# Output-bank copies, weight conversions and token sums emitted at other places in a fused attention and two-layer kernel

## The chip, the cores and the metric

One core of a Trainium2 chip runs the whole program. The metric is the device time of one execution in microseconds (us). The engines are TensorE (PE), VectorE (DVE), ScalarE (ACT), GpSimd (POOL) and SyncE (SP, which issues every DMA here). Each runs its own instructions in the order in which the program emitted them, and waits for semaphores of the others.

## The reference

A linear attention over 4 x 576 tokens (8 heads of 64), then a gated layer, then a softplus layer. All is float32 on the chip.

```python
q_s = softmax over d of q;  k_s = softmax over tokens of k
kv = einsum('bhsd,bhse->bhde', k_s, v);  x = einsum('bhsd,bhde->bhse', q_s, kv)   # 2304 x 512
xn = x / rms(x) * rms_g
x = (silu(xn @ w_gate) * (xn @ w_val)) @ w_out          # 512 -> 1536 -> 512
h = x @ w_in                                            # 512 -> 2048
out = softplus(h) @ w_out2                              # 2048 -> 512
```

## The kernel before

**Arithmetic.** A float32 factor is split in two parts, high and low, and a product is three matmuls (L728 to L730). So every weight and every activation has to be cast (high) and subtracted (low) before PE can use it. Weights arrive as 64-bit floats: a load into one of two `raw` buffers (`fetch`, L211), then a chain of steps on ACT and DVE (`stages`, L340): `convert_a` (absolute value, L246 or L250), `clamp` (L255, L261), `words` (L265, L269; it ends with `fetch(n + RAW)`, the load of the weight two places on), the cast `make_h` (L310 on ACT, L308 on POOL in the softplus layer), the subtraction `make_l` (L316). Weights that come in pairs pass through four sums (L330 to L333).

**Tiles and stages.** Tokens come in six blocks of 384. The first four feature blocks of the gated layer run as plain products in a hand-written list that also does the attention, and, for the last two token blocks, in a loop of eight steps (24 positions, below). The other eight feature blocks run in pairs, on pairs of token blocks, as seven products in place of eight, in 12 *units* (`u`, 0 to 11): each of the seven products is 6 matmuls for the gate and 6 for the value, and its factors are weight sums and *quads*, which are blocks or sums of blocks of the tokens (11, 21, t2, t1, t3, 22, t4). The softplus layer has 24 such units (`u`, 0 to 23), with one product of 6 matmuls each, and output products of 512 columns.

**Quads.** A *run* is a stretch of units on one pair of token blocks; run 0 is unit 0, run 1 is unit 1, run 2 is units 2 and 3. `quad_todo` lists what a run needs in the order of `MAKE`: a `sum` is one DVE subtraction (L986), usually in place over one of its blocks, a `split` is an ACT cast (L1003, L1006) and, at the next position, a low half (`quad_low`, L1016 for a whole place, L1019 twice for a place in two banks), on POOL for runs 1 and 2, else on DVE. A split needs a free place; the head of the list blocks what follows.

**Order of the work.** The emission order is a small planner's. After each half product comes `background(rate)`: one *position*. It adds `rate` to a credit of at most 1.0, emits at most one entry of `quad_todo`, and lets `convert_some` take one step of each conversion in progress (three at most) while the credit isn't negative; steps and sums take credit. `need` forces conversions whose weights are due. A unit of the gated layer has 14 positions, one of the softplus layer 26.

**Output products.** The output products of unit u (8 `parts` of 6 matmuls) are emitted during unit u + 1, one after each product (`more(1)`), the rest at the unit's end. Each part needs one of four PSUM banks that ACT first fills with the residual (`prepare`, L1165), and ACT copies its result out (L1175). A part's emission is followed by the `prepare` of the part two places on. PSUM banks of the gate and value products are freed by ACT copies (L1252), by DVE additions (L1255, then L1259 and ACT's cast L1234 and POOL's low half L1235 for a hidden tile) or, at the seventh product, by the activation L1263. In the softplus layer the addition is L1364. The last plain output (`o_last`) is copied out by DVE (L775).

Of the kernel before, what the change touches and what calls it, by code (L numbers as in the profile page):

```python
# [79 lines left out]
def linear_attention_swiglu_softplus_kernel(  # L80
# [31 lines left out]
    NBITS = 3  # L112
    BW = P
# [80 lines left out]
    raws = {}  # L194
    bits = {}
# [12 lines left out]
    order += pair_a(3)[:4] + pair_b(2, Y0 + Y1) + pair_b(3, H2 + Y0 + Y1) + pair_a(3)[4:]  # L208
# [4 lines left out]
    def fetch(n):  # L213
# [17 lines left out]
        raws[n] = raw  # L231

# [168 lines left out]
    now = [0]  # L401
    credit = [0.0]

    def convert_some(force=False):
        stuck = False
        if not jobs or (len(jobs) < NBITS and jobs[-1][3] > 0):
            n = next_job[0]
            if n < len(order) and n - NBITS not in bits:
                jobs.append([n, list(stages(n)), now[0], 0])
                next_job[0] += 1  # L410
# [327 lines left out]
    with tc.manual_schedule():  # L738
# [197 lines left out]
        apart = {}  # L936
        outside = {}
# [40 lines left out]
        def quad_op(r, what, name):  # L978
            layer, jp = runs[r]
            if what == "sum":  # L980
# [3 lines left out]
                if r == 0 and name in ("t3", "t4"):  # L984
                    apart[r, name] = late[0].tile([P, 2, T], F32, tag="hb", name="t", bufs=NH)
                nc.vector.tensor_tensor(out=block(r, name), in0=x, in1=y, op=ALU.subtract)  # L986
                credit[0] -= 0.9
                return True
# [21 lines left out]
        def quad_low(r, name, src, w, q):  # L1010

            layer, jp = runs[r]
            credit[0] -= 0 if r in (1, 2) else 0.9
# [6 lines left out]
            if layer == "a":  # L1020
# [7 lines left out]
                if r == 0:  # L1028
                    last = {"t2": 1, "t1": 0}.get(name)
                else:  # L1030
                    last = {"t3": 1, "t4": 0}.get(name)
# [3 lines left out]
        quad_todo = []  # L1035
        for r, (layer, jp) in enumerate(runs):
            if layer == "b" or jp not in made_a:
                quad_todo += [(r, *x) for x in MAKE]
            else:
                quad_todo += [(r, "load", x) for x in USE]  # L1040
# [33 lines left out]
        def background(rate, quads=1):  # L1074
            now[0] += 1
            credit[0] = min(credit[0] + rate, 1.0)
# [4 lines left out]
        for i in range(LS, NA):  # L1081
# [10 lines left out]
            background(1.4)  # L1092
# [13 lines left out]
            background(1.4)  # L1106
# [8 lines left out]
            background(1.4)  # L1115
# [4 lines left out]
        def h_tile():  # L1120
            made[0] += 1
            if made[0] % (NH + 2) < NH:
                return late[0].tile([P, 2, T], F32R, tag="hb", name="hb", bufs=NH)
# [19 lines left out]
        def o_last():  # L1143
# [5 lines left out]
            def part(m):  # L1149
                c = slice(m * P, (m + 1) * P)  # L1150
                mm3(acc[m][:, :T], w[:, 0, c], w[:, 1, c], h[:, 0], h[:, 1], False, True)
                x2_out(i, m, "V")
# [70 lines left out]
        for u in range(len(ORDER_A)):  # L1223
# [16 lines left out]
            for k, (wn, off, xname, b, new) in enumerate(SEVEN):  # L1240
# [3 lines left out]
                for n in "gv":  # L1244
# [23 lines left out]
                    if n == "v":  # L1268
                        if ends_run:
                            release(r, xname)  # L1270
                        if u % 3 == 2:
                            done = {1: ("gx1", "vx1"), 4: ("gx3", "vx3"), 5: ("x4",), 6: ("gx2", "vx2")}.get(k, ())
                            for x in done:
                                ring_done((x, p))
                    background(1.1)
                if u % 3 == 1 and k == 0 and u < 3:
                    pass
                more(1)
            more(8)
            if u == 0:  # L1280
                add_ahead(outputs, 2)
# [67 lines left out]
        for u in range(NPB * len(ORDER_B)):  # L1349
# [4 lines left out]
            for k, (wn, off, xname, b, new) in enumerate(SEVEN):  # L1354
# [18 lines left out]
                background(0.45)  # L1373
                more(2 if u == 0 and k < 2 else 1)
                background(0.45, 0)
            for _ in range(12):
                more(1)
                background(0.45, 0)
# [38 lines left out]
```

## Time and profile before

| what | value |
|---|---|
| median of three runs | 969.01 us (965.15 to 969.09) |
| the profiled execution, its span | 969.88 us, 968.1 us |
| PE, DVE, ACT, POOL busy | 902.3, 597.7, 487.4, 239.2 us |
| DMA | 203.5 MB, 210 GB/s over the span |
| mean granted clock of TensorE | 0.978 |

Busy shares are means over stages with different limits. The stage rows below are read first; the waits of PE and the queues around them second. A granted clock of 1.00 is 2.4 GHz; the mean of a stretch lies below it where part of it ran at 1.2 GHz. The "idle before" in a row's brackets is the time in which its engine stood still, with what ended it.

### The profile page before, as it was taken

The numbers are of one execution on the slowest core, as the hardware profiler recorded it, in microseconds if no ns is written. First come the engines' busy times: TensorE is split into PE (matmuls) and PEld (weight loads), VectorE is DVE, ScalarE is ACT, GpSimd is POOL, SyncE is SP. The second block draws the span as 40 slices with busy tenths as digits, with TensorE's granted clock in tenths as the row PEclk, the third lists the DMA queues.
The fourth block names the chain that finished last, engine by engine and source line by source line (L and its number), as shares of the span: only waits on it lengthen the run. The fifth ranks groups of instructions, "written<-read, shape, count | busy, mean of one in ns | idle before, by whom it ended". The sixth has DMA issues, their size and how long they took to land.

```text
span 968.1 us, 13616 instructions
## 1 busy us (share of the span) xinstructions
PE 902.3 (93%) x4840; PEld 842.3 (87%) x4840; DVE 597.7 (62%) x1013; ACT 487.3 (50%) x994; POOL 239.2 (25%) x215
## 2 busy tenths in 40 slices
PE   7799999999677999999999987799999999999997
PEld 7689999999677999899999886689888989898996
DVE  7999987765754788788888877941442223322221
ACT  4585634344456677667777852233443334333332
POOL 4666404111454112121112155761000000000000
PEclk9999999999988999999999998899999999999999
DMA  9974444332557598687597639887539565286501
GB/s 253 252 188 119 122 124 120 120 109 100 221 222 279 189 359 295 219 316 291 178 383 289 226 150 339 300 311 291 174 111 340 163 204 164 101 328 206 167 22 65
DMA packets 111235, 203.53 MB, mean 210 GB/s; under 512 B 30272, under 2 KB 71232, under 8 KB 111168
## 3 DMA queue, kind: packets, MB, share of 16 engines
q1 hardware_dynamic: 111168, 202.67, 62.5%
q8 instruction: 38, 0.62, 0.3%
q14 instruction: 29, 0.24, 0.1%
HBM read 155.19 MB, written 47.45 MB: 209 GB/s over the span
## 4 chain that ended last, share of the span: by engine, by line
PE 67%; DVE 16%; DMA 6%; ACT 5%; issue 4%; POOL 2%; DVEq 0%; SPq 0%; ACTq 0%; POOLq 0%
PE yacc L729 6%; PE yacc L730 6%; PE yacc L728 6%; PE h L730 5%; PE h L729 5%; PE h L728 5%; PE acc L728 4%; PE acc L729 4%; PE acc L730 4%; PE g L728 3%; PE g L730 3%; PE g L729 3%; PE v L728 3%; PE v L729 3%; PE v L730 3%
## 5 line engine op out<-in xcount | busy, mean ns | idle before, releaser
L1364 DVE TENSOR_TENSOR p<-h,p 128x384 f32<-128x384 f32 x72 | 39.9, 555 | 160.6 <-PE h L730 159.0
L728 PE MATMUL h<-quad,wb 128*128 128x384 f32 x336 | 114.1, 339 | 16.8 <-DVE p L1364 15.3
L729 PE MATMUL h<-quad,wb 128*128 128x384 f32 x336 | 114.9, 342 | 0.0
L730 PE MATMUL h<-quad,wb 128*128 128x384 f32 x336 | 114.9, 342 | 0.0
L1298 ACT ACTIVATE p<-p 128x384 f32<-128x384 f32 x72 | 37.8, 526 | 131.9 <-DVE p L1364 131.9
L728 PEld LDWEIGHTS h<-quad,wb 128*128 128x128 f32 x336 | 63.9, 190 | 26.1 <-DVE p L1364 17.0
L1361 ACT COPY p<-h 128x384 f32<-128x384 f32 x72 | 34.6, 481 | 102.8 <-PE h L730 101.8
L728 PE MATMUL yacc<-wb,hb 128*128 128x512 f32 x210 | 82.2, 392 | 1.7 <-ACT y L1314 1.7
L729 PE MATMUL yacc<-wb,hb 128*128 128x512 f32 x210 | 83.0, 395 | 0.0
L730 PE MATMUL yacc<-wb,hb 128*128 128x512 f32 x210 | 83.0, 395 | 0.0
L729 PEld LDWEIGHTS h<-quad,wb 128*128 128x128 f32 x336 | 63.5, 189 | 7.2
L728 PE MATMUL g<-quad,w 128*128 128x384 f32 x168 | 58.1, 346 | 10.8 <-ACT s L1263 6.0
L1235 POOL TENSOR_TENSOR hb<-p,hb 128x384 fp32r<-128x384 f32 x26 | 27.0, 1037 | 154.5 <-ACT hb L1234 115.4
L730 PEld LDWEIGHTS h<-quad,wb 128*128 128x128 f32 x336 | 63.7, 190 | 0.0
L728 PE MATMUL acc<-hb,w 128*128 128x384 f32 x136 | 47.9, 352 | 15.8 <-ACT acc L1165 15.6
L728 PE MATMUL v<-quad,w 128*128 128x384 f32 x168 | 57.9, 345 | 0.5 <-DVE p L1255 0.5
L729 PE MATMUL g<-quad,w 128*128 128x384 f32 x168 | 58.0, 345 | 0.0
L730 PE MATMUL g<-quad,w 128*128 128x384 f32 x168 | 58.0, 345 | 0.0
L729 PE MATMUL v<-quad,w 128*128 128x384 f32 x168 | 57.2, 341 | 0.0
L730 PE MATMUL v<-quad,w 128*128 128x384 f32 x168 | 57.0, 339 | 0.0
L728 PE MATMUL acc<-h,w 128*128 128x384 f32 x152 | 51.2, 337 | 2.8 <-ACT acc L1165 2.8
L269 DVE SCALAR_TENSOR_TENSOR bits<-raw,bits 128x512 int32<-128x512 int32 x62 | 51.5, 833 | 1.6
(202 smaller groups left out, 2503.3 us busy)
## 6 DMA issues: line engine op xcount, KB each, us to landing
wb<-kept SPq DMA_DIRECT2D x120, 512.0 KB, 5.3
quad<-outside SPq DMA_DIRECT2D x31, 768.0 KB, 6.6
kept<-ws SPq DMA_DIRECT2D x40, 512.0 KB, 4.7
raw<-in_moe_w_out_dram SPq DMA_DIRECT2D x26, 512.0 KB, 3.8
outside<-quad SPq DMA_DIRECT2D x13, 768.0 KB, 3.8
quad<-outside SPq DMA_DIRECT2D x22, 384.0 KB, 5.4
raw<-in_moe_w_in_dram SPq DMA_DIRECT2D x16, 512.0 KB, 4.7
outside<-quad SPq DMA_DIRECT2D x16, 384.0 KB, 2.4
```

The source lines that it names most:

```text
L269: nc.vector.scalar_tensor_tensor(out=b, in0=words[:, :, 0], scalar=29, in1=b, op0=ALU.logical_shift_right, op1=ALU.bitwise_or)
L728: nc.tensor.matmul(out=ps, lhsT=wh, rhs=xh, start=first, stop=False, skip_group_check=more)
L729: nc.tensor.matmul(out=ps, lhsT=wh, rhs=xl, start=False, stop=False, skip_group_check=more)
L730: nc.tensor.matmul(out=ps, lhsT=wl, rhs=xh, start=False, stop=last, skip_group_check=more)
L1235: nc.gpsimd.tensor_tensor(out=h[:, 1], in0=a, in1=h[:, 0].bitcast(F32), op=ALU.subtract)
L1298: nc.scalar.activation(out=ln, in_=src, func=AF.Softplus)
L1361: nc.scalar.copy(out=t, in_=bk[b])
L1364: nc.vector.tensor_tensor(out=t, in0=bk[b], in1=t, op=ALU.add)
```

## The change

- `convert_some` starts a conversion only when a clock that `background` advances (2.08 at a plain position, 1.55 in the gated units, 0.6 in the softplus units) has passed its load's emission by `LANDING` = 7.5; a forced start (`need`) doesn't look at it.
- In a gated unit `more(1)` comes after the value's half product and ahead of that position's `background`, in place of after it; the first unit prepares three banks ahead, not two.
- Run 1's sums t1, t3 and t2 are emitted among run 0's entries, behind its first five (in the plain steps); t1 and t2 go to tiles of their own (`hb`) in place of overwriting their blocks. Run 1's splits have a new order, and the place of one token block is freed after the split of 22, not t3.
- A low half on POOL takes 0.6 credit in place of none. The last plain outputs are copied by ACT, not DVE. The weights `y` of the fourth pair come behind its `o` weights in the order.

```diff
@@ -110,6 +110,7 @@
     NS = 3
     NH = 5
     NBITS = 3
+    LANDING = 7.5
     BW = P
     RAW = 2
     EARLY = ["x20", "x21", "x22", "x23", "xy3", "xy2"]
@@ -192,6 +193,7 @@
         ring_free.add(ring_of.pop(key))
 
     raws = {}
+    fetched = {}
     bits = {}
     def pair_a(p):
         return [(n, GA[0] + 2 * p + i) for n in "gvo" for i in range(2)]
@@ -205,7 +207,7 @@
     order = [(n, f) for f in range(GA[0]) for n in "gvo"] + pair_a(0)
     order += pair_a(1) + pair_b(0, H2 + Y0 + Y1)
     order += pair_a(2)[:4] + pair_b(1, H2 + Y0 + Y1) + pair_b(2, H2) + pair_a(2)[4:]
-    order += pair_a(3)[:4] + pair_b(2, Y0 + Y1) + pair_b(3, H2 + Y0 + Y1) + pair_a(3)[4:]
+    order += pair_a(3)[:4] + pair_b(2, Y0 + Y1) + pair_b(3, H2) + pair_a(3)[4:] + pair_b(3, Y0 + Y1)
     for p in range(4, NPB):
         order += pair_b(p, H2 + Y0 + Y1)
     assert len(order) == len(set(order)) == 3 * FA + 2 * FB
@@ -229,6 +231,7 @@
             src = {"g": w_gate, "v": w_val, "h": w2_in}[name]
             nc.sync.dma_start(out=r64.rearrange("p (k c) -> p k c", c=P), in_=src[:, c].rearrange("(k p) c -> p k c", p=P))
         raws[n] = raw
+        fetched[n] = clock[0]
 
     softplus = []
 
@@ -399,13 +402,14 @@
     jobs = []
     next_job = [NL]
     now = [0]
+    clock = [0.0]
     credit = [0.0]
 
     def convert_some(force=False):
         stuck = False
         if not jobs or (len(jobs) < NBITS and jobs[-1][3] > 0):
             n = next_job[0]
-            if n < len(order) and n - NBITS not in bits:
+            if n < len(order) and n - NBITS not in bits and (force or clock[0] >= fetched.get(n, 0.0) + LANDING):
                 jobs.append([n, list(stages(n)), now[0], 0])
                 next_job[0] += 1
         for job in list(jobs):
@@ -934,6 +938,16 @@
         hl_out = [-1, -2, -3]
         hl_rel = {-1, -2, -3}
         apart = {}
+        hb_keys = []
+
+        def hb_tile(key, dtype):
+
+            if len(hb_keys) >= NH:
+                assert hb_keys[-NH] is None or hb_keys[-NH] in split_done, hb_keys
+            hb_keys.append(key)
+            return late[0].tile([P, 2, T], dtype, tag="hb", name="hb", bufs=NH)
+
+        split_done = set()
         outside = {}
 
         def free_place():
@@ -981,10 +995,12 @@
 
                 x, y = {"t1": ("12", "11"), "t3": ("22", "12"), "t2": ("22", "t1"), "t4": ("21", "t2")}[name]
                 x, y = block(r, x), block(r, y)
-                if r == 0 and name in ("t3", "t4"):
-                    apart[r, name] = late[0].tile([P, 2, T], F32, tag="hb", name="t", bufs=NH)
+                if (r, name) in ((0, "t3"), (0, "t4"), (1, "t1"), (1, "t2")):
+                    apart[r, name] = hb_tile((r, name), F32)
                 nc.vector.tensor_tensor(out=block(r, name), in0=x, in1=y, op=ALU.subtract)
                 credit[0] -= 0.9
+                if (r, name) == (1, "t4"):
+                    split_done.add((1, "t2"))
                 return True
             place = free_place()
             if place is None:
@@ -1010,7 +1026,9 @@
         def quad_low(r, name, src, w, q):
 
             layer, jp = runs[r]
-            credit[0] -= 0 if r in (1, 2) else 0.9
+            if (r, name) != (1, "t2"):
+                split_done.add((r, name))
+            credit[0] -= 0.6 if r in (1, 2) else 0.9
             eng = nc.gpsimd if r in (1, 2) else nc.vector
             if w is not None:
                 eng.tensor_tensor(out=w[:, :, 1], in0=src, in1=w[:, :, 0].bitcast(F32), op=ALU.subtract)
@@ -1027,14 +1045,23 @@
 
                 if r == 0:
                     last = {"t2": 1, "t1": 0}.get(name)
+                elif r == 1:
+
+                    last = {"22": 1, "t4": 0}.get(name)
                 else:
                     last = {"t3": 1, "t4": 0}.get(name)
                 if last is not None:
                     free.append(("big", f"xy{2 * jp + last}", now[0]))
 
         quad_todo = []
+        EARLY_SUMS = [(1, "sum", x) for x in ("t1", "t3", "t2")]
+        MAKE_1 = [(1, "split", x) for x in ("11", "t1", "t2", "21")] + [(1, "sum", "t4")] + [(1, "split", x) for x in ("t3", "22", "t4")]
         for r, (layer, jp) in enumerate(runs):
-            if layer == "b" or jp not in made_a:
+            if r == 0:
+                quad_todo += [(r, *x) for x in MAKE[:5]] + EARLY_SUMS + [(r, *x) for x in MAKE[5:]]
+            elif r == 1:
+                quad_todo += MAKE_1
+            elif layer == "b" or jp not in made_a:
                 quad_todo += [(r, *x) for x in MAKE]
             else:
                 quad_todo += [(r, "load", x) for x in USE]
@@ -1071,8 +1098,9 @@
             for m in ms:
                 halves(("a", j), xn[j][:, m * T:(m + 1) * T], m)
 
-        def background(rate, quads=1):
+        def background(rate, quads=1, step=1.55):
             now[0] += 1
+            clock[0] += step
             credit[0] = min(credit[0] + rate, 1.0)
             if quads:
                 advance(quads, True)
@@ -1089,7 +1117,7 @@
             nc.scalar.activation(out=s, in_=g_ps, func=AF.Silu)
             if i == LS + GA[0]:
                 free.append(("hl", now[0]))
-            background(1.4)
+            background(1.4, 1, 2.08)
             next_halves(i, (0, 1))
             v_ps = bank("v", 1, 2)[:, :T]
             kmul(v_ps, wt["v", f], x)
@@ -1103,7 +1131,7 @@
                 free.extend([("hl", now[0])] * 2)
             a = fa.tile([P, T], F32, tag="a", name="a")
             nc.vector.tensor_tensor(out=a, in0=s, in1=v_ps, op=ALU.mult)
-            background(1.4)
+            background(1.4, 1, 2.08)
             h = fa.tile([P, 2, T], F32R, tag="h", name="h")
             nc.scalar.copy(out=h[:, 0], in_=a)
             nc.gpsimd.tensor_tensor(out=h[:, 1], in0=a, in1=h[:, 0].bitcast(F32), op=ALU.subtract)
@@ -1112,7 +1140,7 @@
                 o_step(i - 1)
                 if j == NB - 1 and f:
                     ring_done(("o", f - 1))
-            background(1.4)
+            background(1.4, 1, 2.08)
 
         hbs = {}
         made = [0]
@@ -1120,7 +1148,7 @@
         def h_tile():
             made[0] += 1
             if made[0] % (NH + 2) < NH:
-                return late[0].tile([P, 2, T], F32R, tag="hb", name="hb", bufs=NH)
+                return hb_tile(None, F32R)
             return fa.tile([P, 2, T], F32R, tag="h", name="h")
 
         def seven(ps, w, off, x, first):
@@ -1149,7 +1177,7 @@
             def part(m):
                 c = slice(m * P, (m + 1) * P)
                 mm3(acc[m][:, :T], w[:, 0, c], w[:, 1, c], h[:, 0], h[:, 1], False, True)
-                x2_out(i, m, "V")
+                x2_out(i, m, "A")
                 if m == KD - 1:
                     ring_done(("o", stepsA[i][2]))
 
@@ -1272,13 +1300,12 @@
                             done = {1: ("gx1", "vx1"), 4: ("gx3", "vx3"), 5: ("x4",), 6: ("gx2", "vx2")}.get(k, ())
                             for x in done:
                                 ring_done((x, p))
+                    if n == "v":
+                        more(1)
                     background(1.1)
-                if u % 3 == 1 and k == 0 and u < 3:
-                    pass
-                more(1)
             more(8)
             if u == 0:
-                add_ahead(outputs, 2)
+                add_ahead(outputs, 3)
             if u % 3 == 0:
                 need(("o0", p), ("o1", p))
             add_fill(outputs)
@@ -1370,12 +1397,12 @@
                     activate(u, 0, 1, c[2], c[2])
                 elif k == 6:
                     activate(u, 1, 0, bk[0], fa.tile([P, T], F32, tag="a", name="c21"))
-                background(0.45)
+                background(0.45, 1, 0.6)
                 more(2 if u == 0 and k < 2 else 1)
-                background(0.45, 0)
+                background(0.45, 0, 0.6)
             for _ in range(12):
                 more(1)
-                background(0.45, 0)
+                background(0.45, 0, 0.6)
             for x in ("hx1", "hx3", "hx2", "hx4"):
                 ring_done((x, "b", u))
             if u + 2 < NPB:
```

## Rows read from the trace of the kernel before

**Rows 1.** Windows by stage: us, busy us (instructions) by engine, PE clock, DMA share, GB/s.

```profile
239.46:269.00 29.54, 18.71 (x98) 17.81 (x97) 22.35 (x32) 14.83 (x30) 13.62 (x12) 0.89 0.58 223
269.00:304.65 35.65, 27.64 (x132) 25.27 (x133) 21.28 (x27) 21.32 (x46) 20.96 (x15) 0.88 0.63 238
304.65:551.24 246.59, 236.15 (x1322) 232.63 (x1321) 197.06 (x332) 175.22 (x392) 44.90 (x42) 0.98 0.76 277
551.24:645.00 93.76, 76.38 (x369) 68.26 (x369) 70.72 (x87) 35.90 (x74) 58.35 (x52) 0.93 0.73 265
```

**Rows 2.** Timeline of PE, units 0 and 1: start us, us, line, operation, idle before.

```profile
252.98 0.33 PE L728 MATMUL v<-quad,w 128*128 128x384 f32 x1
...
253.85 0.34 PE L730 MATMUL v<-quad,w 128*128 128x384 f32 x1
259.06 0.58 PE L728 MATMUL g<-quad,w 128*128 128x384 f32 x1 [4.87 <-DVE p L1255]
...
268.99 0.69 PE L728 MATMUL g<-quad,w 128*128 128x384 f32 x1 [5.96 <-ACT s L1263]
...
273.77 0.45 PE L728 MATMUL acc<-hb,w 128*128 128x384 f32 x1 [0.67 <-ACT acc L1165]
```

**Rows 3.** Waits of PE, whole span: us in total, times, longest us.

```profile
PE acc L728 <- ACT acc L1165: 18.4, 15, 3.3
PE h L728 <- DVE p L1364: 15.3, 4, 6.6
```

**Rows 4.** Timeline of DVE in unit 0.

```profile
249.36 1.75 DVE L986 TENSOR_TENSOR xn<-xn 128x768 f32<-128x768 f32 x1 [3.47 <-POOL quad L1016]
...
256.65 0.55 DVE L775 COPY x<-acc 128x384 f32<-128x384 f32 x1
257.12 0.95 DVE L986 TENSOR_TENSOR xn<-xn 128x768 f32<-128x768 f32 x1
...
258.45 0.55 DVE L1255 TENSOR_TENSOR p<-g,p 128x384 f32<-128x384 f32 x1
```

**Rows 5.** Windows of 25 us, one of the plain steps, columns as in rows 1.

```profile
200.00:225.00 25.00, 25.00 (x146) 25.00 (x145) 16.45 (x28) 9.85 (x22) 4.33 (x4) 1.00 0.28 95
```

**Rows 6.** Timeline of POOL, units 0 and 1.

```profile
246.51 1.01 POOL L1235 TENSOR_TENSOR hb<-p,hb 128x384 fp32r<-128x384 f32 x1 [6.47 <-ACT hb L1234]
247.48 1.85 POOL L1016 TENSOR_TENSOR quad<-xn,quad 128x768 fp32r<-128x768 f32 x1
249.28 5.80 POOL L1019 TENSOR_TENSOR quad<-xn,quad 128x384 fp32r<-128x384 f32 x4
...
263.20 2.40 POOL L1019 TENSOR_TENSOR quad<-xn,quad 128x384 fp32r<-128x384 f32 x2
...
268.85 3.62 POOL L1016 TENSOR_TENSOR quad<-xn,quad 128x768 fp32r<-128x768 f32 x2
272.41 1.02 POOL L1235 TENSOR_TENSOR hb<-a,hb 128x384 fp32r<-128x384 f32 x1
```

**Rows 7.** Timeline of ACT in unit 1, the cast of run 1's last block.

```profile
272.50 0.83 ACT L1003 CAST quad<-xn 128x768 fp32r<-128x768 f32 x1 [2.43 <-POOL quad L1016]
```

**Rows 8.** Timeline at the end of unit 2, ACT and PE.

```profile
328.76 0.48 ACT L1165 COPY acc<-x 128x384 f32<-128x384 f32 x1
329.17 0.49 ACT L1263 ACTIVATE s<-g 128x384 f32<-128x384 f32 x1
...
329.29 0.44 PE L728 MATMUL acc<-hb,w 128*128 128x384 f32 x1 [1.55 <-ACT acc L1165]
```

**Rows 9.** Waits of DVE, units 2 to 11.

```profile
DVE ws L316 <- ACT ws L310: 8.6, 12, 1.1
```

**Rows 10.** Timeline of DVE in the softplus layer.

```profile
595.22 0.69 DVE L246 SCALAR_TENSOR_TENSOR bits<-raw 128x512 f32<-128x512 f32 x1 [5.11 <-DMA raw<-in_moe_w_in_dram]
...
600.04 0.55 DVE L1364 TENSOR_TENSOR p<-h,p 128x384 f32<-128x384 f32 x1
```

**Rows 11.** Groups of DVE, 605 to 624.5 us: operation xcount | busy us, mean ns | idle before.

```profile
L246 DVE SCALAR_TENSOR_TENSOR bits<-raw 128x512 f32<-128x512 f32 x3 | 3.4, 1117 | 0.3 <-DMA raw<-in_moe_w_in_dram 0.3
```

## What I predict, and how it follows from the rows

> **What bounds the kernel now.** I read the stages first, then who TensorE waits for, then the engine queues around each long wait. In the stage table the columns to compare are PE busy, the granted clock and the length. From 645 us on PE is busy for practically the whole time, and before 239 us the emission list is untouched, so nothing can be won there. The four stages between lose time in different ways [rows 1]. Matmuls of 384 columns start 0.174 us apart at the full clock (five steps from 252.98 to 253.85) [rows 2]. Unit 0 of the seven-product layer (84 product matmuls and 12 of the last plain output) needs 96 x 0.174 = 16.7 us, a later unit (84 + 48) 22.9 us. Units 0 and 1 take 239.46 to 304.65 = 65.2 us where 39.6 would do: 25.6 lost. Units 2 to 11 take 246.6 us where 229 would do: 17.6 lost. In the first softplus units PE is idle for 93.8 - 76.4 = 17.4 us, and with a mean clock of 0.93 up to 0.07 x 93.8 = 6.6 us more goes to half speed (1.2 in place of 2.4 GHz) [rows 1]. In all some 67 us of 969.9 can be touched.
>
> The waits view says who is late: the copy of the residual into an output bank, 18.4 us in 15 waits, and DVE's addition in the softplus layer, 15.3 us in 4 [rows 3]. The two long holes at the entry are a DVE addition (4.87 us) and the gate activation on ACT (5.96 us) [rows 2]. None of these is work that PE lacks data for; each is a queue that stands still in front of it.
>
> **The change part by part.**
>
> *Token sums of run 1 moved into the plain steps, two of them no longer in place.* In unit 0 DVE sat 3.47 us waiting for POOL, because the first sum overwrote a block whose low half POOL was still reading; then came three sums, a pair sum of weights and output copies before the addition at 258.45 that freed PE [rows 4]. The change takes the three sums (the first 1.75, the last 0.95, the middle one between) with the 3.47 us, and three copies of 0.55 ahead of the addition, out of that stretch of DVE's queue: 9 us or more, against a lateness of 4.87. That hole closes. The sums now run in plain steps, at positions where the list was blocked for lack of a place; DVE was busy 16.45 of 25 us there and PE 25 of 25 [rows 5]; I cost them at nothing, and if the cover were gone at 3 x 0.95 to 1.75, 3 to 5 us. The four copies go to ACT at about 0.48 us, 1.9 us in a unit in which ACT was busy 14.8 of 29.5 [rows 1].
>
> What is late next is POOL. It makes the low halves of run 1 and of the hidden tiles. From 246.51, where it starts, to 273.4, where it ends the half that the first output part of unit 0 needs [rows 6], its work is four halves of 1.0, 1.85 for the first block, 5.80 for two blocks in single-bank places, 2.40 for a third, 3.62 for two whole ones: 17.7 us; the other 9.2 of those 26.9 us it idles, behind the two holes. The new order moves one block past that half, so that the same sort of work (four halves, three blocks in single places, three whole) comes ahead of it. Fed without a gap it ends at 246.5 + 16.5 to 17.7 = 263 to 264.2. ACT has the same floor: its cast of the last block, which stood 2.43 us behind POOL at 272.50 [rows 7], takes the place that the POOL read of the block before it frees, and the bank copies are queued behind it. So PE reaches the first output part at about 264.2 in place of 273.77 [rows 2]: 9.5 us. By its own work it would be there at 239.5 + 16.7 + 2.1 = 258.3, so it still stands some 6 us; before, it stood as long and then ran 12 matmuls at half speed, which after the change falls behind 264.2 rather than ahead of it: 12 x 0.174 at half the clock = 2.1 back. Net 7.4, bounds 3 and 10.
>
> *Unit 1* had 10.1 us more to lose after that part (304.65 - 273.77 less 20.8). Four bank waits and two half-speed stretches make it, behind an ACT that waited for DVE. Three copies ahead give each copy one more product and part, 3.1 us, which is more than all but one of these waits. I leave 3 us for DVE operations beside POOL and take 7, bounds 0 and 10.
>
> *Bank copies in units 2 to 11.* A wait falls once a unit, at the last part. The case at 329.29 shows what is under it: the copy ended at 329.24, but the gate activation that frees the next product's bank started right behind it at 329.17 and lasts 0.49 [rows 8]. With the copy made earlier PE goes through that part (1.04 us) and then waits for the activation: of 1.55 us only 1.04 - 0.41 = 0.63 is won. Ten such units are 6.3 us. The half speed after these waits (0.02 x 246.6 = 4.9 at most [rows 1]) goes in part. Against it, the part's own output copy now waits on ACT for the part's matmuls before the conversion casts get their turn: 1.04 - 0.48 = 0.56 us for three products a unit (at the others ACT waits longer for DVE anyway), and DVE's 12 waits of 8.6 us for those casts [rows 9] grow by up to 1.5 each. ACT is busy 175 of 247 us and DVE 197 [rows 1], so it fits. I take 6 for both together, bounds 14 won and 8 lost.
>
> *Conversions held back.* A load that DVE has not got stops its whole queue: at 595.22 it had stood 5.11 us for one, and the addition that PE needed came at 600.04 behind that conversion [rows 10].  In softplus units there are 26 positions to 16 us; 7.5 of clock at 0.6 is 13 positions, 8 us, so this wait goes, or shrinks to what a slow landing leaves. The second 6 us hole has another cause: between 605 and 624.5 three conversions follow each other, each first step 1.12 us in place of the 0.69 at 595.22 [rows 10, 11]. The hold spaces them, since each load is issued by the conversion two before it: by hand, one start every 8 to 9 positions in place of 3.2 in a unit of 26, alternating. Price of the hold: counted from position to position, one to two conversions more are left when softplus begins (before, ten and a half), where POOL makes their halves; they have room until the last weights are due three units later. In the swiglu units the hold is 5 positions, 8.8 us, and no weight is forced by my count, though the third output pair ends on the very position at which it is due; forced, it would cost a load's wait and a conversion, some 10 us. Of the 17.4 idle and 6.6 of clock I take 11, bounds 0 and 19.
>
> *The rest.* Two weights of the fourth output pair come two places earlier, which covers the hold there. The credit for POOL's halves only delays conversions while POOL is full. Neither has a price of its own.
>
> Sum: 7.4 + 7 + 6 + 11 = 31.4. The profiled execution took 969.9 us (span 968.1 and 1.8 around it), 0.9 over the median, so 938.5 profiled and 937.6 for a median; I say 938.
>
> **The rivals.**
>
> *Softplus keeps its holes.* The second hole stood with only 0.3 us of DMA wait in its stretch, so DVE's own work is enough to make it; with two conversions more and POOL beside it the spacing may only move it. For it: DVE is busy 70.7 of 93.8 us there [rows 1]. Against: the waits come from bunches of three. Price 11: 949.
>
> *POOL holds DVE in units 0 and 1.* The same sum took 1.75 us beside POOL and 0.95 alone [rows 4]. POOL, now without gaps, would do this to some nine DVE operations with two SBUF inputs a unit, 7 us in a unit; the 7 us of unit 1 stay lost: 945. The Trainium skill, "SBUF — State Buffer", section "Who interferes with whom", has this as an exclusive lock that whoever starts first keeps for a whole instruction; the row at 249.36 agrees in kind.
>
> *It does only the entry.* Bank copies and loads only hand their waits to the next in the queue; 14.4 won: 955.
>
> *All of it goes,* clock included, with POOL's floor alone left: 969.9 - 9.5 - 10 - 14 - 18 = 918.
>
> *ACT falls into step with PE (slower).* Each output copy now stands on ACT for its part, and behind it stand the casts, halves and gates. If its 0.56 us surfaces at every product of 77 it is 43 us, and 969.9 - 25.4 + 43 = 987; it decides from 25.4/77 = 0.33 us a product. For it: DVE's evacuation sits behind casts already [rows 9]. Against: 29% of ACT's time there is free. The Trainium skill, "TensorE: Matmul & The Clock Gate", section on the array of 32x32 parts, says ACT's queue is strictly first in, first out; the gate at 329.17, right behind a copy it doesn't need, agrees.
>
> **How the numbers follow.** Forecast 0.50, softplus 0.16, POOL and DVE 0.10, entry alone 0.08, all of it 0.06, ACT slower 0.06, gains and losses cancelling 0.04. Range: the forecast's bounds taken together are some 10 either way, 928 to 948; down to 924 and up to 956 it takes in three of the rivals and leaves out all of it, the slower case, the cancelling one and small tails, under 0.2. Chances at half a per cent (4.8 us, what a measurement here can tell): faster 0.88, same 0.05, slower 0.07.
>
> **What would show it.** In the changed profile: no wait of PE on the addition of product four in unit 0, and one wait at the first output part near 258 to 264 that ends with POOL; bank copies gone from the top of PE's waits, with the gate activation in their place at under 0.7 us a unit; no DVE wait over 2 us on a raw load; conversions 8 to 9 positions apart in softplus. Wrong, if ACT shows waits on its output copies of over 0.3 us a product, if a bunch of forced conversions stands at a unit's end, or if PE's waits on DVE's addition in softplus keep over 10 us.

## The result, and the profile after

The changed kernel takes 961.79 us (median of eight executions, 958.60 to 965.34) against 971.01 for the kernel before on the same chip (eight, 965.15 to 973.10). The ratio is 0.9914, with a 95% interval of 0.9888 to 0.9939: faster, by about 9 us where 31 were forecast, and above the upper end of the range. The profiled execution has a span of 958.9 us against 968.1.

The windows view of the changed kernel, with the same stages as [rows 1] (units 0, 1, 2 to 11, and the start of the softplus layer):

```profile
240.41:266.13 25.72, 17.36 (x98) 16.40 (x97) 19.49 (x25) 16.57 (x35) 14.24 (x12) 0.95 0.81 307
266.13:295.25 29.12, 25.77 (x132) 24.68 (x132) 13.68 (x22) 20.11 (x44) 19.76 (x15) 0.93 0.53 204
295.25:534.62 239.37, 233.34 (x1320) 229.85 (x1320) 188.60 (x323) 173.18 (x389) 47.37 (x43) 0.99 0.79 285
534.62:640.00 105.38, 84.14 (x387) 75.53 (x388) 85.27 (x103) 37.95 (x80) 64.08 (x58) 0.90 0.76 274
```

The first two lines together are 54.8 us (before 65.2), the third 239.4 (before 246.6). The fourth is longer than the window of before, because the stage it samples has grown. Measured from its first unit to the start of its seventh, where PE runs through again, the softplus stage takes 124.7 us against 116.8. The ledger of the profiled executions, in us:

| stage | before | after | measured | forecast |
|---|---|---|---|---|
| up to unit 0 | 239.5 | 240.4 | +0.9 | 0 |
| entry, units 0 and 1 | 65.2 | 54.8 | -10.4 | -14.4 |
| units 2 to 11 | 246.6 | 239.4 | -7.2 | -6 |
| softplus units 0 to 5 | 116.8 | 124.7 | +7.9 | -11 |
| the rest, to the last matmul | 294.0 | 293.6 | -0.4 | 0 |
| span | 968.1 | 958.9 | -9.2 | -31.4 |

So 18.9 of the 22.2 us that are missing were lost in one place, the softplus units, and 4.0 at the entry.

Who PE waits for in the whole span of the changed kernel (us in total, times, longest):

```profile
PE h L732 <- DVE p L1391: 18.9, 4, 6.4
PE g L732 <- ACT s L1291: 11.2, 5, 5.8
...
PE v L732 <- DVE p L1283: 1.5, 1, 1.5
```

The bank copy that led [rows 3] with 18.4 us is gone from the list altogether. The gate activation (L1291, before L1263) has come up instead (6.0 us in one wait before), and the softplus addition (L1391, before L1364) has grown from 15.3 to 18.9 us.

Lines are some 3 to 28 higher than before. The spread to read stages by: in nine kernels below whose entry is that of the changed kernel, it took 54.3 to 55.8 us; with all else alike, units 2 to 11 still differed by up to 2.5 us, nearly all of it in unit 2 (27.4 to 29.5 us), while units 3 to 10 agreed within 0.3 us each.

### The profile page after: what moved, and what is told of

The parts are those of the page before. It is cut to its first block, busy times and chain, and to the rows that moved or that the text cites. A ratio compares the mean times of both kernels' runs of the same rounds, so it can differ in the third digit from the quotient of the medians.

```text
span 958.9 us, 13523 instructions
## 1 busy us (share of the span) xinstructions
PE 900.7 (94%) x4840; PEld 841.8 (88%) x4840; DVE 596.1 (62%) x1006; ACT 484.4 (51%) x992; POOL 245.4 (26%) x220
## 4 chain that ended last, share of the span: by engine, by line
PE 66%; DVE 15%; ACT 6%; issue 4%; POOL 3%; DMA 3%; SPq 2%; DVEq 0%; POOLq 0%; ACTq 0%
PE yacc L733 6%; PE yacc L734 6%; PE yacc L732 6%; PE h L734 5%; PE h L733 5%; PE h L732 5%; PE acc L733 4%; PE acc L734 4%; PE acc L732 4%; PE g L732 3%; PE v L732 3%; PE g L734 3%; PE g L733 3%; PE v L734 3%; PE v L733 3%
## 5 line engine op out<-in xcount | busy, mean ns | idle before, releaser
L1391 DVE TENSOR_TENSOR p<-h,p 128x384 f32<-128x384 f32 x72 | 40.0, 555 | 157.8 <-PE h L734 151.2
L732 PE MATMUL h<-quad,wb 128*128 128x384 f32 x336 | 115.6, 344 | 22.4 <-DVE p L1391 18.9
L733 PE MATMUL h<-quad,wb 128*128 128x384 f32 x336 | 116.0, 345 | 0.0
L734 PE MATMUL h<-quad,wb 128*128 128x384 f32 x336 | 116.0, 345 | 0.0
L732 PEld LDWEIGHTS h<-quad,wb 128*128 128x128 f32 x336 | 64.7, 193 | 32.2 <-DVE p L1391 20.7
L733 PEld LDWEIGHTS h<-quad,wb 128*128 128x128 f32 x336 | 64.6, 192 | 7.3
L732 PE MATMUL g<-quad,w 128*128 128x384 f32 x168 | 57.8, 344 | 13.1 <-ACT s L1291 11.2
L1263 POOL TENSOR_TENSOR hb<-p,hb 128x384 fp32r<-128x384 f32 x26 | 29.1, 1118 | 139.7 <-ACT hb L1262 96.3
L734 PEld LDWEIGHTS h<-quad,wb 128*128 128x128 f32 x336 | 64.6, 192 | 0.0
L734 PE MATMUL g<-quad,w 128*128 128x384 f32 x168 | 56.6, 337 | 0.0
L733 PE MATMUL g<-quad,w 128*128 128x384 f32 x168 | 56.6, 337 | 0.0
L272 DVE SCALAR_TENSOR_TENSOR bits<-raw,bits 128x512 int32<-128x512 int32 x62 | 54.6, 884 | 1.6
L268 DVE SCALAR_TENSOR_TENSOR bits<-raw,bits 128x512 int32<-128x512 int32 x62 | 52.0, 841 | 0.9
```

The costliest lines, as they stand in the source:

```text
L268: nc.vector.scalar_tensor_tensor(out=b, in0=words[:, :, 1], scalar=-0x40000000, in1=b, op0=ALU.bitwise_and, op1=ALU.bitwise_or)
L272: nc.vector.scalar_tensor_tensor(out=b, in0=words[:, :, 0], scalar=29, in1=b, op0=ALU.logical_shift_right, op1=ALU.bitwise_or)
L732: nc.tensor.matmul(out=ps, lhsT=wh, rhs=xh, start=first, stop=False, skip_group_check=more)
L733: nc.tensor.matmul(out=ps, lhsT=wh, rhs=xl, start=False, stop=False, skip_group_check=more)
L734: nc.tensor.matmul(out=ps, lhsT=wl, rhs=xh, start=False, stop=last, skip_group_check=more)
L1263: nc.gpsimd.tensor_tensor(out=h[:, 1], in0=a, in1=h[:, 0].bitcast(F32), op=ALU.subtract)
```

## The experiments

All stage lengths come from each kernel's profiled execution; "left" counts the conversions whose first step belongs to the softplus part. Ratios are to the kernel before on the same chip, with 95% intervals.

| kernel | entry | units 2-11 | softplus 0-5 | left | ratio |
|---|---|---|---|---|---|
| before | 65.2 | 246.6 | 116.8 | 10 | 1 |
| after | 54.8 | 239.4 | 124.7 | 12 | 0.9914 (0.9888 to 0.9939) |
| e6_sums_only | 57.0 | 245.8 | 118.3 | 10 | 0.9927 (0.9910 to 0.9944) |
| e5_banks_only | 63.8 | 247.4 | 118.7 | 10 | 1.0007 (0.9983 to 1.0031) |
| e11_no_bank_order | 56.5 | 238.4 | 126.4 | 12 | 0.9913 (0.9894 to 0.9933) |
| e2_hold_only | 65.1 | 253.7 | 122.1 | 11 | 1.0135 (1.0108 to 1.0161) |
| e1_no_hold | 55.8 | 249.1 | 117.8 | 10 | 0.9930 (0.9908 to 0.9952) |
| e3_hold_gated_only | 55.7 | 240.8 | 129.2 | 12 | 0.9953 (0.9938 to 0.9968) |
| e4_hold_softplus_only | 54.9 | 248.0 | 118.9 | 10 | 0.9927 (0.9902 to 0.9952) |
| e9_hold_4.5 | 54.9 | 247.2 | 118.4 | 10 | 0.9935 (0.9920 to 0.9950) |
| e13_slow_no_hold | 54.3 | 243.6 | 128.4 | 12 | 0.9944 (0.9924 to 0.9964) |
| e14_no_loads | 54.9 | 243.4 | 115.2 | 10 | 0.9859 (0.9825 to 0.9893) |
| e7_casts_on_act | 55.7 | 241.9 | 118.9 | 12 | 0.9851 (0.9813 to 0.9889) |
| e8_no_pool_halves | 54.8 | 239.5 | 115.0 | 12 | 0.9800 (0.9758 to 0.9841) |
| e10_run1_low_on_dve | 51.8 | 238.1 | 125.5 | 12 | 0.9827 (0.9790 to 0.9865) |
| e12_combined | 51.8 | 248.2 | 116.6 | 10 | 0.9862 (0.9845 to 0.9879) |
| e15_two_moves | 51.8 | 238.9 | 120.2 | 12 | 0.9804 (0.9761 to 0.9848) |

### Which part earns the time

**Token sums alone**: the changed kernel without the hold, the bank order and the new place of the fourth pair's weights.

```diff
-  ... and (force or clock[0] >= fetched.get(n, 0.0) + LANDING)
-  pair_b(3, H2) + pair_a(3)[4:] + pair_b(3, Y0 + Y1)
+  pair_b(3, H2 + Y0 + Y1) + pair_a(3)[4:]
-  add_ahead(outputs, 3)
+  add_ahead(outputs, 2)
   (more(1) back behind the two tiles, last plain copy back on DVE)
```

> The kernel before with the token sums, run 1's order of splits and the credit for POOL's halves alone; no hold, bank copies as before, last plain output by DVE. If the sums make the entry's gain: 56 to 57.5 us from unit 0 to unit 2 (65.2 before, 54.8 changed, bank copies alone 63.8), the rest as before, ratio 0.990 to 0.993. If sums and bank copies are needed together: 60 us or more, 0.996.

Ratio 0.9927: alone they give what the whole change gives, within the intervals. The entry takes 57.0 us, 8.2 of the 10.4 won there.

**Bank copies alone**, in the kernel before.

```diff
-  x2_out(i, m, "V")
+  x2_out(i, m, "A")
   for n, ... :
+      if n == "v":
+          more(1)
       background(1.1)
-  more(1)
-  add_ahead(outputs, 2)
+  add_ahead(outputs, 3)
```

> The kernel before with the bank copies three ahead and in front of background, and the last plain output copied by ACT; no hold, no sums moved. If the bank copies win by themselves what I forecast: units 2 to 11 at 241 us (before 246.6), unit 1 some 7 us shorter. If they win only together with the hold, because ACT then no longer stands in front of loads that haven't landed: units 2 to 11 at 247 to 250 us, as without the hold in the changed kernel, and a ratio of 0.995 to 1.002.

No change: 1.0007. The kernel before had 9 waits on the bank copy in units 2 to 11, 10.4 us in all:

```profile
PE acc L728 <- ACT acc L1165: 10.4, 9, 2.2
```

In this one PE waits there, between the first product of unit 2 and the first softplus product, for:

```profile
PE g L728 <- ACT s L1263: 6.5, 4, 2.1
PE h L728 <- ACT s L1263: 2.1, 1, 2.1
PE acc L728 <- ACT hb L1234: 1.7, 1, 1.7
PE acc L729 <- POOL hb L1235: 0.6, 1, 0.6
```

That is 10.9 us, of which 8.6 are on the gate activation. (A further 5.4 us on it stand ahead of the first product of unit 2 and so belong to unit 1.)

DVE waits for ACT's weight casts (in the kernel before, 8.6 us for `ws` [rows 9] and 6.8 for `w`):

```profile
DVE ws L316 <- ACT ws L310: 15.2, 15, 1.9
DVE w L316 <- ACT w L310: 11.9, 11, 1.9
```

The wait went whole to later instructions in ACT's queue, most of it to the gate activation, and the casts behind the bank copies became later.

**The change without the bank order** is the counter-test: `background(1.1)`, then `more(1)` after both tiles, and `add_ahead(outputs, 2)`.

> The changed kernel with the bank copies back where they were: two ahead, behind background. If they only hand their wait to the gate activation: units 2 to 11 at 239 to 242 us, unit 1 at most 3 us longer, ratio 0.990 to 0.995. If the hold wins there only together with them: 244 us or more, ratio 0.997 or more.

Same time as the change (0.9913), units 2 to 11 at 238.4 against 239.4. PE's waits in units 2 to 11, counted as above, first of this kernel, then of the changed one:

```profile
PE acc L732 <- ACT acc L1193: 5.4, 7, 1.6
```

```profile
PE g L732 <- ACT s L1291: 2.7, 3, 1.3
PE h L732 <- ACT s L1291: 1.9, 1, 1.9
PE v L732 <- DVE a L1294: 1.2, 2, 1.1
```

It is 5.4 us on the bank copy, or 5.8 us on the gate activation and on the product that DVE makes of its result (L1294). Only the entry shows something for the bank order, 56.5 against 54.8, hardly more than its spread.

**The hold alone**, in the kernel before (its order of weights kept).

```diff
-  if n < len(order) and n - NBITS not in bits:
+  if n < len(order) and n - NBITS not in bits and (force or clock[0] >= fetched.get(n, 0.0) + LANDING):
   (with fetched, clock and the steps of the change)
```

> The kernel before with the hold alone. Theory A: two conversions more are left when softplus begins, some 7 us lost there and 1 to 3 us won in the gated units: ratio 1.004 (1.000 to 1.009). Theory B: DVE's 5 us load wait and ACT's 4 us of load waits go, nothing is lost: ratio 0.990 or less.

Slower, 1.0135. Unit 10 alone takes 36.7 us where its neighbours take 23 to 25. PE at that unit's first output part:

```profile
507.94 0.69 PE L732 MATMUL acc<-h,w 128*128 128x384 f32 x1 [8.60 <-ACT w L313]
509.70 0.69 PE L734 MATMUL acc<-h,w 128*128 128x384 f32 x1 [0.75 <-DVE w L319]
```

The output weights of the fourth pair were not made when they were due. The forecast had priced such a forced conversion at some 10 us, for the third pair; here it cost about 13. In the change the two weights of the fourth pair that moved behind its output weights prevent it. No run has the change with the old order of weights, but by the order of its instructions that kernel would force the same conversions at the end of unit 9, and the change forces none.

### What the hold does

**The change without it**: the condition on `clock[0]` taken out.

> The changed kernel with its hold taken out: a conversion starts as soon as its turn comes, all else as changed. Theory A (the hold leaves two conversions more for the softplus units, where DVE beside POOL can't carry them): the softplus part has ten conversions again and is back at the 417 us that it took before, with the wait for a late load; entry and bank copies keep their 16 to 17 us: ratio to before 0.983 (0.979 to 0.988). Theory B (the hold spares DVE its load waits, and something else lost the softplus time): the load waits of ACT and DVE come back, ratio 0.995 or more.

0.9930, within the interval of the change, and between the ratios of the two theories. Its stages differ: units 2 to 11 take 9.7 us more, the softplus units 6.9 less. So most of what the hold wins in the one stage it loses in the other: 12 conversions are left for the softplus part, without it 10.

**Only in the gated units** (`force or softplus or ...`) and **only in the softplus units** (`force or not softplus or ...`).

> The changed kernel with the hold in the plain and gated units alone, none in the softplus units. Theory A: the two conversions are left over all the same, and start in bunches: as the changed kernel or up to 3 us slower, ratio 0.991 to 0.995. Theory B: the load waits in softplus come back, ratio 0.997 or more. If the spacing in softplus is itself what costs: 0.985.

> The changed kernel with the hold in the softplus units alone. Theory A: ten conversions are left; spaced or not, DVE needs the same time for each: as without any hold, ratio 0.983 (0.979 to 0.988). If spacing helps as I predicted it: 0.975. Theory B: softplus as in the changed kernel, ACT's load waits in the gated units back: 0.994 or more.

With ten conversions left, the hold in softplus does nothing (118.9 against 117.8), and the ratio stays that of no hold, not the 0.983 of theory A. With twelve it does help, 124.7 against 129.2. The two conversions more cost (129.2 - 117.8)/2 = 5.7 us each without it and (124.7 - 118.9)/2 = 2.9 with it. They were counted rightly in the forecast, and priced at nothing.

**A shorter hold**, `LANDING = 4.5`.

> The changed kernel with a hold of 4.5 in place of 7.5. By the order of its instructions ten conversions are left for the softplus units, as before the change, not twelve. If what is left over is what the hold costs: softplus units 0 to 5 at 117 to 119 us (124.7), and units 2 to 11 at 240 to 244 us if a hold of three positions still keeps DVE and ACT off most late loads: ratio 0.984 to 0.988. If the long hold is what wins the gated units: 246 us there and ratio 0.991 or more.

Ten are left, and units 2 to 11 keep 247.2 us. A hold that moves no conversion wins next to nothing there.

**Is it the moved work or the spacing?** One kernel moves the two conversions by a slower credit and no hold (`background(0.98)` for `background(1.1)` in the gated units). The other keeps ten left and takes the loads' waits away, by giving later conversions the tiles of earlier loads (`if n >= 26: raws[n] = first_raw[n % 2]; return`).

> The changed kernel without a hold, and 0.98 credit a position in the gated units in place of 1.1, so that by the order of its instructions twelve conversions are left for softplus, as with the hold of 7.5. Theory C (the hold wins the gated units by leaving two conversions out of them): units 2 to 11 at 239 to 242 us, softplus units 0 to 5 at 125 to 129, ratio 0.993 to 0.998. Theory D (it wins them because DVE and ACT no longer stand in front of loads): units 2 to 11 at 246 to 249 us, softplus as above, ratio 1.000 or more.

> The changed kernel without a hold, and the weight loads from the 27th on left out: every later conversion takes the words that the 25th and 26th load brought, so nothing waits for a load. Ten conversions are left for softplus. Theory C: units 2 to 11 stay at 246 to 249 us; ratio 0.990. Theory D: 239 to 241 us there. In softplus: if load waits still cost anything there, units 0 to 5 under 114 us (117.8 without a hold); if DVE's own work makes the holes, 115 or more.

243.6 and 243.4, from 249.1 without a hold, to 239.4 with it: each gives some 5.5 of the 9.7 us, and lies between the lengths that its two theories gave. Unit by unit neither repeats the hold. With it, units 3 to 5 are 1.3 to 1.6 us shorter each. Without loads, units 3 to 6 take what they take without a hold, within 0.03 us, and units 7, 10 and 11 win 2.5, 1.0 and 1.1. The slower credit wins 3.7 of its 5.5 us in unit 2, which varies most from kernel to kernel, and loses 3.0 in unit 6. So without a hold late loads cost some 4.6 us outside unit 2; how the rest of the hold's gain divides between moved work and spacing isn't shown. In softplus the loads are not what hurts: with none of them the stage still takes 115.2 us against 117.8, PE still waits 11.6 us for the addition, and slowing the credit instead of holding leaves 128.4.

### What makes the conversions long in softplus

**The high halves on ACT** instead of POOL (in `make_h`, always `nc.scalar.copy`), and then **POOL without any weight half**: there the low halves are plain copies on ACT, and their subtraction is left out.

> The changed kernel with the softplus units' weight casts on ACT in place of POOL. If DVE's conversion steps are stretched by POOL: fewer long steps, softplus units 0 to 5 at 119 us in place of 124.7, ratio 0.986. If it is the number of DVE steps alone: 124 us, 0.991.

> As the run before it, and the weights' low halves in the softplus units left out: ACT copies the weight into their place, so POOL has only the hidden tiles' halves. If POOL stretches DVE: the five steps of a conversion take 2.9 to 3.2 us in place of 5, softplus units 0 to 5 at 103 to 108 us, ratio 0.972 to 0.977. If the number of DVE steps is what counts: 118 us or more, 0.985.

The casts on ACT take the stage from 124.7 to 118.9 with twelve left, as expected of a stretch by POOL. Without POOL's halves it is 115.0, between the two expectations: ACT makes all those copies on top, and PE now waits for ACT's copy of the product.

```profile
PE h L731 <- ACT p L1387: 11.5, 4, 4.6
```

Deferred conversions still have a price with the casts on ACT: twelve left against ten (e7 and e15 against e12) cost 1.2 to 1.8 us each, though the holds differ too. DVE's groups in the softplus stage, line by line (xcount | busy us, mean ns | idle before), in the changed kernel:

```profile
L272 DVE SCALAR_TENSOR_TENSOR bits<-raw,bits 128x512 int32<-128x512 int32 x13 | 14.0, 1079 | 0.4
L268 DVE SCALAR_TENSOR_TENSOR bits<-raw,bits 128x512 int32<-128x512 int32 x13 | 13.7, 1055 | 0.4
L249 DVE SCALAR_TENSOR_TENSOR bits<-raw 128x512 f32<-128x512 f32 x12 | 12.2, 1018 | 2.4 <-DMA raw<-in_moe_w_in_dram 2.3
L258 DVE TENSOR_SCALAR bits<-bits 128x512 f32<-128x512 f32 x13 | 11.9, 917 | 0.3
L264 DVE TENSOR_SCALAR bits<-bits 128x512 int32<-128x512 int32 x13 | 11.4, 879 | 0.4
```

and without POOL's weight halves:

```profile
L272 DVE SCALAR_TENSOR_TENSOR bits<-raw,bits 128x512 int32<-128x512 int32 x13 | 10.5, 811 | 0.4
L268 DVE SCALAR_TENSOR_TENSOR bits<-raw,bits 128x512 int32<-128x512 int32 x13 | 10.4, 800 | 0.4
L249 DVE SCALAR_TENSOR_TENSOR bits<-raw 128x512 f32<-128x512 f32 x12 | 9.1, 760 | 12.0 <-DMA raw<-in_moe_w_out_dram 8.5 <-DMA raw<-in_moe_w_in_dram 3.5
L258 DVE TENSOR_SCALAR bits<-bits 128x512 f32<-128x512 f32 x13 | 9.1, 701 | 0.3
L264 DVE TENSOR_SCALAR bits<-bits 128x512 int32<-128x512 int32 x13 | 5.6, 427 | 0.4
```

The same 64 steps take 63.2 us in the one and 44.7 in the other. DVE even waits 12.0 us for loads in the second, five times as long, in a stage that is 9.7 us shorter: here a wait for a load cost little.

### What holds the entry, and a faster kernel

**Run 1's low halves on DVE.**

```diff
-  credit[0] -= 0.6 if r in (1, 2) else 0.9
-  eng = nc.gpsimd if r in (1, 2) else nc.vector
+  credit[0] -= 0.6 if r == 2 else 0.9
+  eng = nc.gpsimd if r == 2 else nc.vector
```

> The changed kernel with run 1's low halves on DVE in place of POOL. If POOL is what is late in units 0 and 1, directly or by stretching DVE: entry (first product of unit 0 to first of unit 2) at 45 to 50 us in place of 54.8, ratio 0.985. If DVE's own work is the bound there: 54 us or more, with the wait in front of DVE additions.

The entry falls to 51.8, between the two expectations, and the ratio to 0.9827, below the whole interval of the change. (Of the 4.6 us between the two profiled executions, 960.65 and 956.05, 3.1 are the entry's. The edit also raises the credit that such a half takes.) POOL, now with one half a product, idles 6.69, 8.44 and 3.17 us between its tiles in unit 0. PE still has its wait:

```profile
262.52 0.69 PE L732 MATMUL g<-quad,w 128*128 128x384 f32 x1 [6.20 <-ACT s L1291]
```

So POOL had a part, 2.6 us of unit 0 (25.7 to 23.1), but it is not the floor there.

**Both moves together**, once with a hold of 4.5, once with that of the change.

> The changed kernel with three changes at once: hold 4.5, run 1's low halves on DVE, softplus weight casts on ACT. If the costs are separate, each as measured: entry 51.7, units 2 to 11 240 to 244, softplus units 0 to 5 112 to 115: ratio 0.973 to 0.979.

> The changed kernel with its hold of 7.5, run 1's low halves on DVE and the softplus weight casts on ACT. If the two costs are separate: entry 51.7, units 2 to 11 238 to 242, softplus units 0 to 5 119: ratio 0.975 to 0.980.

The moves of e10 and e7 on the change as it stands give 0.9804, median 952.11 us against 970.47: faster than both kernels, and at the edge of what was expected. Each keeps its stage (entry 51.8; softplus 120.2 from 124.7). With the shorter hold the forecast was missed, 0.9862: softplus is shorter still, 116.6, but units 2 to 11 go back to 248.2 where 240 to 244 were expected.

## Why the prediction was right and wrong

**The direction, and most of the wait in unit 0: right.** The sums left DVE's queue as worked out, and alone they win what the whole change wins. PE's hole on product four's addition is 1.05 us instead of 4.87 [rows 2]. It was to close; what is left, with a new hole of 1.50 at the value half of the product that waits, stands behind pair sums stretched beside POOL and a wait for POOL's half (the last line). DVE in unit 0 of the changed kernel:

```profile
250.96 1.23 DVE L333 TENSOR_TENSOR sums<-bits 128x256 f32<-128x256 f32 x1
252.22 1.13 DVE L334 TENSOR_TENSOR bits<-bits 128x256 f32<-128x256 f32 x1
...
254.54 1.11 DVE L336 TENSOR_TENSOR sums<-bits,sums 128x256 f32<-128x256 f32 x1
255.58 0.55 DVE L1283 TENSOR_TENSOR p<-g,p 128x384 f32<-128x384 f32 x1
257.51 0.96 DVE L1000 TENSOR_TENSOR xn<-xn,hb 128x768 f32<-128x768 f32 x1 [1.39 <-POOL quad L1037]
```

**The first output part at 264.2: wrong, it came at 270.14.** Counted from the start of unit 0, that is 4.6 us won where 7.4 were forecast. The failing step is "fed without a gap". POOL, in units 0 and 1:

```profile
255.34 2.14 POOL L1037 TENSOR_TENSOR quad<-xn,quad 128x384 fp32r<-128x384 f32 x2
260.23 1.00 POOL L1263 TENSOR_TENSOR hb<-p,hb 128x384 fp32r<-128x384 f32 x1 [2.75 <-ACT hb L1262]
261.19 1.80 POOL L1034 TENSOR_TENSOR quad<-xn,quad 128x768 fp32r<-128x768 f32 x1
265.03 1.43 POOL L1263 TENSOR_TENSOR hb<-p,hb 128x384 fp32r<-128x384 f32 x1 [2.04 <-ACT hb L1262]
```

It idles 2.75 and 2.04 us behind ACT's cast, which waits for DVE. The forecast wait for POOL at the first output part doesn't come. PE stands 5.82 us for the gate activation, one product earlier, about as long as before (5.96):

```profile
256.18 0.45 PE L732 MATMUL g<-quad,w 128*128 128x384 f32 x1 [1.05 <-DVE p L1283]
...
259.00 0.44 PE L732 MATMUL v<-quad,w 128*128 128x384 f32 x1 [1.50 <-DVE p L1283]
...
266.13 0.69 PE L732 MATMUL g<-quad,w 128*128 128x384 f32 x1 [5.82 <-ACT s L1291]
...
270.14 0.42 PE L732 MATMUL acc<-hb,w 128*128 128x384 f32 x1
```

What is late, as the traces read, is the chain addition, activation or copy, addition, cast that runs between DVE and ACT for each product and has no output part beside it yet, together with the weight casts and quads in the same two queues. The kernel with POOL nearly idle keeps 6.20 us of it; no run took anything else off that chain, so that it is the floor is argued and not shown. I had summed one engine's work and taken the sum as the floor, while that engine waited for two others. The rival in which POOL holds DVE was seen in kind: each of the four pair sums above took 1.1 to 1.2 us, and with run 1's halves on DVE 0.42 to 0.43.

```profile
249.33 0.42 DVE L333 TENSOR_TENSOR sums<-bits 128x256 f32<-128x256 f32 x1
```

Moving the halves won 3.1 us at the entry.

**Unit 1**, counted as in the forecast from the first output part on, gave 5.8 us (30.9 to 25.1) against 7.

**Up to unit 0** the prediction called the emission list untouched, although its own sums, and the hold, work there. The stage took 0.9 us more, which says little: in the kernels above it ends between 238.0 and 241.9 us, in no order.

**Bank copies in units 2 to 11: the term of 0.63 us a unit was mis-sized; it is 0.** The mechanism was named (the gate activation stands right behind the copy [rows 8]), and the sign set for it came, under 0.7 us of such waits a unit. But I let PE keep the part it runs through meanwhile, as if the activation stayed where it was. The two kernels with the hold show 5.4 us on the copy or 5.8 on the activation and its product, the two without it 10.4 or 10.9, and DVE's waits for the casts grew from 15.4 to 27.1 us when the copies moved alone. That this stage came near its forecast, -7.2 for -6, is chance: the hold made it, to which I had given nothing there.

**The hold in softplus: wrong sign.** The wait for a load did shrink, 5.4 to 2.4 us of DVE's idle time before L249 (the forecast allowed none over 2; one of 2.12 is left). What fell is the next step, that spaced conversions leave room for the addition. They are spaced about as forecast (by the order of the instructions, 6 to 9 positions from the fourth on; before, 1 to 17), yet each lasts about as long as the space. DVE, and then PE:

```profile
581.95 0.79 DVE L249 SCALAR_TENSOR_TENSOR bits<-raw 128x512 f32<-128x512 f32 x1 [2.12 <-DMA raw<-in_moe_w_in_dram]
582.78 1.37 DVE L258 TENSOR_SCALAR bits<-bits 128x512 f32<-128x512 f32 x1
...
585.98 0.55 DVE L1391 TENSOR_TENSOR p<-h,p 128x384 f32<-128x384 f32 x1
586.72 0.69 DVE L249 SCALAR_TENSOR_TENSOR bits<-raw 128x512 f32<-128x512 f32 x1 [0.19 <-DMA raw<-in_moe_w_in_dram]
...
590.07 1.65 DVE L272 SCALAR_TENSOR_TENSOR bits<-raw,bits 128x512 int32<-128x512 int32 x1
591.83 0.56 DVE L1391 TENSOR_TENSOR p<-h,p 128x384 f32<-128x384 f32 x1
```

```profile
586.58 0.69 PE L732 MATMUL h<-quad,wb 128*128 128x384 f32 x1 [6.36 <-DVE p L1391]
```

From 581.95 to 591.72 DVE does two conversions and, between them, the addition at 585.98; PE, which it let go on at 586.58, had stood 6.36 us by then. Beside POOL the five steps of a conversion take some 4.9 us of DVE's time (63.2 us for 64 steps), and each conversion that is deferred costs PE 2.9 us with the hold and 5.7 without. The row that should have told me is in [rows 11], 1.12 us a first step. I read it as the sign of a bunch, but over the whole softplus stage of the kernel before all ten of them average 1.09 us, and without POOL's weight halves 0.76. The sign set for being wrong, over 10 us of waits on the addition, was met with 18.9. The step that failed in so many words is "they have room until the last weights are due". The rival "softplus keeps its holes" had the cause but stopped at zero; it did not ask what the two conversions more would cost.

**The rivals.** "Only the entry", 955, came nearest: 969.9 - 10.4 = 959.5 of entry, and the rest cancels to within 1.2 of the 960.65 us of the profiled execution. That is luck in part: units 2 to 11 won 7.2 us and softplus lost 7.9, neither of which it foresaw. ACT in step with PE did not come: ACT's waits on its output copies are 2.6 us in ten units, and a unit takes 23.0 to 23.9 us in eight of them, where 22.9 is the count of matmuls.

**Open**: what is left of the holes in softplus. The shortest still take 115 us for units whose sequel runs at 15.8 each. Without POOL's halves PE waits there on ACT, without loads on DVE, so more than one chain is near the edge; which comes first after both was not tried.

## What to carry to other kernels

A wait taken from one instruction of a first-in first-out queue is won only as far as nothing behind it in that queue is late too: look up when the next instruction would have ended, and do not count the work between the two as won. Holding background work back moves it; before it is free, find the stage that receives it and price it there, with durations from that stage. An engine's summed work is a floor only if its inputs don't wait for other engines; where two others hand a tile to and fro, price that round trip too.

## What the runs showed of the hardware

DVE steps with a single SBUF input were stretched beside POOL too, not only those with two. The two such steps of a conversion, L258 and L264 (TENSOR_SCALAR on 128x512), averaged 917 and 879 ns beside POOL's weight halves, and 701 and 427 without them; the two-input L272 went from 1079 to 811. The Trainium skill, "SBUF — State Buffer", section "Who interferes with whom", counts tensor_scalar among the operations that can enter a two-port mode and then contend with GpSimd for an exclusive lock; both rows agree. I had reckoned with two-input operations alone.
